# Attention and a gated layer in windows: the second window's weights in another order, its sums kept in SBUF, copies a step later, tiles moved to multiples of 512 bytes

## The chip, the core and the metric

One core of a Trainium2 chip runs one program. The metric is the device time of that program in microseconds (us); lower is better. TensorE (PE) multiplies, VectorE (DVE) and ScalarE (ACT) work on tiles in SBUF and PSUM, GpSimd (POOL) and SyncE (SP) here mostly issue DMA transfers between DRAM and SBUF. Each engine takes its instructions strictly in the order of its own queue and waits where an input isn't there.

## The reference

Linear attention on 8 batches of 576 tokens with 8 heads of 64, then a gated layer on the 4608 token rows of 512:

```python
q_s = softmax(q, axis=-1); k_s = softmax(k, axis=2)       # k: over the 576 positions
kv = np.einsum('bhsd,bhse->bhde', k_s, v)
x = np.einsum('bhsd,bhde->bhse', q_s, kv)                   # then laid out as [4608, 512]
gate = 1.0 / (1.0 + np.exp(-(x @ w_gate)))                  # w_gate, w_val: [512, 1536]
out = gate * (x @ w_val) @ w_out                            # w_out: [1536, 512]
```

The weights come in as 64-bit floats and are narrowed to 32 bits on the chip.

## The kernel before

The tokens are cut into 9 windows of 512 (w = 0 to 8; the title's spans). The columns of the gate and value weights are cut into 12 blocks j of 128, or 6 pairs p of two blocks.

Window 0 runs in 12 steps j with plain float32 matmuls. In step j, `g1_0(j)` (L594) makes gate and value columns in two PSUM tiles `gv` out of a ring of three; `g_sig_0` (ACT, L602) takes the sigmoid of the one, `g_mul_0` (DVE, L606) multiplies it by the other, which frees the tiles for the steps after; and `g2_0(j-1)` (PE, L621) multiplies the result of the step before with the output weights. Beside it, three kinds of work prepare the windows to come. Weights are narrowed: `w_low` and `w_join` on DVE (L131, L153), `w_top` on ACT (L138, L146), the same as `wo_low`, `wo_join`, `wo_top` for the output weights. `wo_save(j)` splits the output weights of step j into a high part (ACT copy, L195) and a low part (DVE subtraction, L196), both fp32r, in a tile `wo_hl` (two buffers in turn), and POOL saves them to DRAM. `w_sums(p)` (DVE, L226) and `split_w(p)` (ACT casts L213, DVE subtractions L214) form for a pair four sums S1 to S4 of weight blocks, for a scheme with seven instead of eight block products, and split sums and three plain blocks (`a_w`, kept in SBUF) into high and low parts. The sums of a pair are put in the one buffer `s_sb` and saved to DRAM; those of the last pair go through `wo_hl` instead. And `after_first(j)` runs the attention of window 1: maxima, exponentials and sums of k and q (`k_max`, `k_sub`, `k_exp`, `k_sum`, `qn_max`, `qn_sub`, `qn_exp`, `qn_sum`, `qf_mul`), `k_mm` and `k_done` for kv, transposes `qf_tr`, splits `qT_split`, `x_mm` and its evacuation `x_ev`, and at the end `c_subs` and `c_split`, which make the moving operands `c_hl` of the window.

Windows 1 to 8 have 6 steps p each. `g1(w, p)` (L639) makes seven products of 12 matmuls of 256 columns, in the order A11, S1, S2, A12, S3, S4, A22: three take their weights (the stationary operand) from `a_w`, four from `s_sb`; ACT and DVE empty PSUM into `sg` (L657 is the first copy). After each S product, `s_load` fetches that sum of the next step into `s_sb` (POOL, L260). `g2` (L702) makes 24 matmuls of 512 columns with the split products `h` as weights and `wo_hl` as moving operand; `wo_load` (POOL, L208) fetches `wo_hl` under two tags, one buffer pair that is called `wo_hl` and one called `wo_t`. `side_a` and `side_b` run the attention of the next window. Window 2's v tiles 2 to 4 take tiles of the `ring` of eleven 2 KB tiles; in the other windows they lie in `f_last`, which in window 0 holds the last pair's weights.

The order of every engine's work is the order in which the code is written (the scheduler is set to manual). The order of windows 1 to 8 is p = 0 to 5 in each.

As the program is built, nearly all large tiles start 64 or 0 bytes past a multiple of 128: `s_sb`, `kv_sb`, `f_last` and `ring` at 128 modulo 512 bytes of a partition, `c_hl`, `a_w`, `h`, `wo_hl` and `wo_t` at 448.

Of the kernel before, what the change touches and what calls it, by code (L numbers as in the profile page):

```python
# [51 lines left out]
def attn_moe(ctx: ExitStack, tc: tile.TileContext, qf, qn, qT, k, kT, v, wg, wv, wo, out):  # L52
# [138 lines left out]

    def wo_save(j):
        src = wo_t[j // 2][:, j % 2]
        t = two.tile([P, 2, DM], F32R, name="wo_hl")
        nc.scalar.copy(out=t[:, 0], in_=src)  # L195
# [55 lines left out]

    def s_save(p, src, i0, i1):
        n = 2 * DM
        nc.gpsimd.dma_start(
            out=s_dram[p][:, i0 * n:i1 * n], in_=src.rearrange("p s h e -> p (s h e)").bitcast(F32)
        )
# [437 lines left out]
    def g2(w, p):  # L694
        if p == 0:
            acc_new(w)
        h, o = h_hl.pop((w, p)), wo_hl.pop((w, p))
        for i in range(2):
            for m in range(NT):
                sl = slice(m * P, (m + 1) * P)  # L700
                for lh, rh in ((0, 0), (0, 1), (1, 0)):
                    nc.tensor.matmul(  # L702
                        acc[w][m], lhsT=h[lh][:, i, sl], rhs=o[i][:, rh],
                        start=(p == 0 and i == 0 and lh == 0 and rh == 0),
                        stop=(p == NS - 1 and i == 1 and lh == 1),
                    )
# [91 lines left out]
    def after_first(j):  # L800
# [17 lines left out]
        if j == 3:
            for hp in range(NP):
                k_sum(1, hp)  # L820
            for c in range(NC):
                qn_sum(1, c)
# [4 lines left out]
        if j == 4:
            k_done(1)
        if 4 <= j <= 7:
            qf_tr(1, j - 4, ps_gv.tile([P, T], F32, name="gv"))  # L830
        if 5 <= j <= 8:
            qT_split(1, j - 5)
# [246 lines left out]
```

## Time and profile before

| | |
|---|---|
| median of 3 runs | 1014.23 us (1014.09 to 1016.1) |
| profiled execution | 1016.99 us, of which the span from first to last instruction is 1015.2 us |
| mean granted TensorE clock | 0.975 |
| window 0 begins its first matmul L594 at | 35.29 us |
| window 1 begins at | 196.49 us |
| window 2 begins at | 317.21 us |

Rows of the trace give the start in us from the span's start, the duration, engine, line, operation, tiles (output <- inputs), shapes and how many instructions are merged in the row; in brackets stands the idle time of the engine before it and what ended that. Rows of stretches (from:to) give the length and then, engine by engine in the order PE, weight loads, DVE, ACT, POOL, the busy time with the number of instructions, then the granted clock, the DMA share and GB/s. A matmul's duration overlaps the next one's, so the pace of matmuls is read from start to start. Lines L are those of the kernel before.

### The profile page before, as it was taken

To read this page: it belongs to the slowest core of one execution; us is meant where nothing else is said; L and a number is where in the kernel's file an instruction comes from. 1 tells how busy PE (TensorE), PEld (TensorE's weight loads), DVE (VectorE), ACT (ScalarE), POOL (GpSimd) and SP (SyncE) were. 2 spreads that over 40 slices of the span, in tenths; PEclk is the share of its full clock that TensorE was granted. 3 is DMA by queue.
4 is the path that set the end of the run, shared out by engine and by line. 5 is a ranking of instruction groups with operands and counts; after the bars stand their busy time and mean duration, and the time that the engine had idled before them with its cause. 6 is when DMAs were issued, how large, how long until landed. Compare 5 with 4: busy or idle time off the path is not lost.

```text
span 1015.2 us, 15663 instructions
## 1 busy us (share of the span) xinstructions
PE 957.5 (94%) x6062; PEld 826.2 (81%) x6062; DVE 611.1 (60%) x1010; ACT 475.9 (47%) x815; POOL 171.2 (17%) x323
## 2 busy tenths in 40 slices
PE   5959899878899999999999999999999999999998
PEld 4525344468799999999999999999999999999997
DVE  8476967566266656666666656665665475464342
ACT  3639887345154535363446344633463344353222
POOL 0000001121112211211122111211221122212120
PEclk8979999979799999999999999999999999999999
DMA  9837756889569996899699968996999679868672
GB/s 334 320 106 272 267 222 172 309 266 339 153 207 208 371 322 205 230 365 313 199 248 358 310 200 262 353 300 203 277 340 275 214 203 340 244 184 249 205 208 83
DMA packets 94873, 259.88 MB, mean 256 GB/s; under 512 B 15376, under 2 KB 17680, under 8 KB 94160
## 3 DMA queue, kind: packets, MB, share of 16 engines
q0 software_dynamic: 44720, 170.42, 54.7%
q1 hardware_dynamic: 50080, 88.48, 29.3%
q8 instruction: 48, 0.79, 0.4%
q14 instruction: 25, 0.20, 0.1%
HBM read 230.29 MB, written 28.56 MB: 255 GB/s over the span
## 4 chain that ended last, share of the span: by engine, by line
PE 76%; DMA 8%; ACT 8%; DVE 5%; issue 3%; POOL 1%; SPq 0%; POOLq 0%; DVEq 0%; ACTq 0%
PE gv L639 43%; PE acc L702 22%; PE gv L594 3%; PE at L362 3%; DMA kmax_row<-k_max 2%; PE acc L621 2%; PE gv L522 2%; ACT ring L341 1%; DMA s<-s_sb 1%; ACT ring L441 1%; DMA q_m_row<-q_m 1%; DMA ring<-v_in 1%; DMA ring<-qT_in 1%; ACT kt L295 1%; DMA q_b<-q_m_row 1%
## 5 line engine op out<-in xcount | busy, mean ns | idle before, releaser
L639 PE MATMUL gv<-c_hl,s_sb 128*128 128x256 f32 x2304 | 283.0, 278 | 12.3 <-ACT sg L657 12.2
L639 PEld LDWEIGHTS gv<-c_hl,s_sb 128*128 128x128 f32 x2304 | 272.5, 189 | 14.7 <-ACT sg L657 14.1
L702 PE MATMUL acc<-wo_hl,h 128*128 128x512 f32 x1152 | 272.8, 393 | 0.0
L702 PEld LDWEIGHTS acc<-wo_hl,h 128*128 128x128 f32 x1152 | 214.7, 189 | 43.7 <-issue 0.2
L639 PE MATMUL gv<-c_hl,a_w 128*128 128x256 f32 x1728 | 231.9, 284 | 0.0
L639 PEld LDWEIGHTS gv<-c_hl,a_w 128*128 128x128 f32 x1728 | 220.2, 192 | 4.1 <-issue 1.0
L260 POOL DMA_DIRECT2D s_sb<-s x192 | 102.2, 533 | 327.1 <-PE gv L639 321.5
L665 DVE TENSOR_TENSOR sg<-gv,sg 128x512 f32<-128x512 f32 x48 | 33.2, 691 | 177.7 <-PE gv L639 177.7
L208 POOL DMA_DIRECT2D wo_hl<-wo x96 | 51.1, 533 | 310.4 <-PE acc L702 307.7
L594 PE MATMUL gv<-x,f_w 128*128 128x512 f32 x160 | 72.7, 607 | 9.5 <-ACT h L602 5.6
L667 ACT COPY sg<-gv 128x512 f32<-128x512 f32 x48 | 28.2, 587 | 107.0 <-PE gv L639 107.0
L657 ACT COPY sg<-gv 128x512 f32<-128x512 f32 x48 | 28.0, 584 | 97.7 <-PE gv L639 73.3
L594 PEld LDWEIGHTS gv<-x,f_w 128*128 128x128 f32 x160 | 30.4, 194 | 47.4 <-issue 34.4
L669 DVE TENSOR_TENSOR sg<-sg 128x512 f32<-128x512 f32 x48 | 33.2, 693 | 57.1 <-ACT sg L667 57.1
L621 PE MATMUL acc<-wo_t,h 128*128 128x512 f32 x96 | 47.3, 639 | 14.1 <-DVE h L606 14.1
L690 DVE TENSOR_TENSOR h<-sg,h 128x1024 fp32r<-128x1024 f32 x48 | 58.8, 1226 | 1.6
L672 ACT ACTIVATE sg<-sg 128x512 f32<-128x512 f32 x48 | 30.4, 632 | 54.0 <-DVE sg L671 54.0
L678 DVE TENSOR_TENSOR sg<-sg 128x512 f32<-128x512 f32 x48 | 33.2, 693 | 33.5 <-ACT sg L672 33.5
L621 PEld LDWEIGHTS acc<-wo_t,h 128*128 128x128 f32 x96 | 19.3, 205 | 40.4 <-issue 23.8
L662 ACT COPY sg<-gv 128x512 f32<-128x512 f32 x48 | 28.2, 587 | 44.4 <-PE gv L639 44.4
L659 ACT COPY sg<-gv 128x512 f32<-128x512 f32 x48 | 28.1, 586 | 26.1 <-PE gv L639 26.0
L396 ACT CAST kv_sb<-kmax_b 64x256 fp32r<-64x256 f32 x14 | 5.7, 404 | 66.5 <-DVE kmax_b L372 66.1
(155 smaller groups left out, 1056.1 us busy)
## 6 DMA issues: line engine op xcount, KB each, us to landing
s_sb<-s POOLq DMA_DIRECT2D x192, 512.0 KB, 7.1
wo_hl<-wo POOLq DMA_DIRECT2D x96, 512.0 KB, 5.7
s<-s_sb POOLq DMA_DIRECT2D x5, 2048.0 KB, 8.1
out<-x SPq DMA_DIRECT2D x36, 256.0 KB, 8.8
ring<-k_in SPq DMA_DIRECT2D x28, 256.0 KB, 14.3
ring<-qn_in SPq DMA_DIRECT2D x28, 256.0 KB, 10.4
q_b<-q_m_row SPq DMA_DIRECT2D x56, 128.0 KB, 8.7
ring<-qT_in SPq DMA_DIRECT2D x28, 256.0 KB, 9.0
```

The costliest lines, as they stand in the source:

```text
L208: nc.gpsimd.dma_start(out=t.rearrange("p h e -> p (h e)"), in_=wo_dram[2 * p + i].bitcast(F32R))
L260: nc.gpsimd.dma_start(out=s_sb[:, i].rearrange("p h n e -> p (h n e)"), in_=s_dram[p][:, i * n:(i + 1) * n].bitcast(F32R),)
L362: nc.tensor.matmul(kvps[b][:, hp], lhsT=kt[:n, sl], rhs=vt[:n, sl], start=(t == 0 and hp == 0), stop=(t == len(KTILES) - 1 and hp == NP - ...
L594: nc.tensor.matmul(ps[n], lhsT=w[:, kt // 2, sl], rhs=x_0[:, kt], start=(kt == 0), stop=(kt == NK - 1),)
L621: nc.tensor.matmul(acc[0][m], lhsT=h_0[j][:, m * P:(m + 1) * P], rhs=wo_t[j // 2][:, j % 2], start=(j == 0), stop=(j == NJ - 1),)
L639: nc.tensor.matmul(ps[:, n], lhsT=lh(kt), rhs=c_hl[i][:, x, kt], start=(first and n == 0 and kt == 0 and lh is wh and x == 0), stop=(last ...
L665: nc.vector.tensor_tensor(out=sg[:, 0], in0=rr, in1=sg[:, 0], op=ALU.add)
L669: nc.vector.tensor_tensor(out=sg[:, 3], in0=sg[:, 3], in1=sg[:, 2], op=ALU.add)
L672: nc.scalar.activation(sg[:, 0:2, 0], sg[:, 0:2, 0], AF.Sigmoid)
L678: tt(out=sg[:, 0:2, 0], in0=sg[:, 0:2, 0], in1=sg[:, 0:2, 1], op=ALU.mult)
L690: nc.vector.tensor_tensor(out=lo, in0=sg[:, :, 0], in1=hi.bitcast(F32), op=ALU.subtract)
L702: nc.tensor.matmul(acc[w][m], lhsT=h[lh][:, i, sl], rhs=o[i][:, rh], start=(p == 0 and i == 0 and lh == 0 and rh == 0), stop=(p == NS - 1 ...
```

## The change

- Window 1 takes its pairs in the order 5, 0, 1, 2, 3, 4 (`step`), the output weights likewise. The last pair's sums go to `s_sb` like the others and are still there when window 1 begins with that pair; they are saved to DRAM from there.
- `split_w(p)` and `w_sums(p)` have fixed steps: sums in even steps, split in the odd step after; the last split is in step 11.
- The high copy of the output weights (`wo_hi`) and `wo_save` run one step later, `wo_low` one step earlier; `wo_top(j+1)` stays in step j but stands ahead of the sigmoid there.
- The attention of window 1 is spread otherwise over the steps (`after_first`, `beside_first`); `x_ev`, `k_done` and `qT_split` stand at the head of a step, before the narrowing.
- Window 2's v tiles 2 to 4 lie in `f_last`, loaded in step 11.
- Three unused tiles shift the others: every tile named above now starts at a multiple of 512 bytes, except the buffer pair called `wo_hl`, which as built starts at 192 modulo 512.

```diff
+    pad = ctx.enter_context(tc.tile_pool(name="pad", bufs=1))
+    pad.tile([P, 80], F32, name="pad_2")
...
+    const.tile([P, 96], F32, name="pad_0")
     s_sb = const.tile([P, 4, 2, 2, 2 * P], F32R, name="s_sb")
...
+    const.tile([P, 48], F32, name="pad_1")
...
+    wo_out = {}
+    def wo_hi(j):
+        wo_out[j] = t = two.tile([P, 2, DM], F32R, name="wo_hl")
+        nc.scalar.copy(out=t[:, 0], in_=wo_t[j // 2][:, j % 2])
+
     def wo_save(j):
-        src = wo_t[j // 2][:, j % 2]
-        t = two.tile([P, 2, DM], F32R, name="wo_hl")
-        nc.scalar.copy(out=t[:, 0], in_=src)
+        t = wo_out.pop(j)
         nc.vector.tensor_tensor(
...
         for i, t in enumerate(s_32.pop(p)):
-            if p < NS - 1:
-                o = s[:, i:i + 1]
-            else:
-                o = two.tile([P, 1, 2, DM], F32R, name="wo_hl", tag="wo_hl")
-            parts(o, t)
-            if p == NS - 1:
-                s_save(p, o, i, i + 1)
-        if p < NS - 1:
-            s_save(p, s, 0, 4)
+            parts(s[:, i:i + 1], t)
+        nc.gpsimd.dma_start(
+            out=s_dram[p], in_=s_sb.rearrange("p s h n e -> p (s h n e)").bitcast(F32)
+        )
...
+    def step(w, i):
+        return (i - 1) % NS if w == 1 else i
...
+    def beside_first(j):
+        if j == 6:
+            k_done(1)
+        if 7 <= j <= 10:
+            x_ev(1, j - 7)
+        if 6 <= j <= 9:
+            qT_split(1, j - 6)
...
             if t < 2:
                 vt = v_two[t]
-            elif b == 2:
-                vt = ring.tile([P, DM], F32, name="ring")
             else:
                 vt = f_last[:, t - 2].rearrange("p n e -> p (n e)")
...
         if j == 10:
+            c_subs()
+            load_next(1, 5, range(2))
             for i in (B11, T1, T2, B21):
                 c_split(i)
-            load_next(1, 5)
-            for i in range(4):
-                s_load(0, i)
+        if j == 11:
+            for t in range(2, 5):
+                v_load(2, t)
...
     for j in range(NJ):
         g1_0(j)
+        beside_first(j)
+        if j > 0:
+            wo_hi(j - 1)
         if j + 2 < NJ:
             w_top(j + 2)
         if j + 1 < NJ:
             w_join(j + 1)
+        if j + 1 < NJ:
+            wo_top(j + 1)
         wo_join(j)
...
-        if j + 1 < NJ:
-            wo_low(j + 1)
+        if j + 2 < NJ:
+            wo_low(j + 2)
         g_sig_0(j)
-        wo_save(j)
+        if j > 0:
+            wo_save(j - 1)
...
-        if j - 1 in sums:
-            split_w(sums[j - 1])
-        if j + 1 < NJ:
-            wo_top(j + 1)
-        if j in sums:
-            w_sums(sums[j])
+        if j % 2:
+            split_w(j // 2)
+        else:
+            w_sums(j // 2)
```

The steps j of window 0 in which `after_first` issues the attention of window 1:

| work | before | after |
|---|---|---|
| qn_max, qn_sub, qn_exp, qn_sum | 0, 1, 2, 3 | 1, 2, 2, 3 |
| k_max (with its trip through DRAM) | 0 | 0 |
| k_sub, k_exp, k_sum | 1, 2, 3 | 3, 4, 2 |
| qf_mul, k_mm | 3, 3 | 4, 5 |
| qf_tr, x_mm (one a step) | 4 to 7, 6 to 9 | 5 to 8, 6 to 9 |
| c_subs | 9 | 10 |

What stands on the engines' queues at three places. First DVE in steps 0 and 1 of window 0, before (f_w, wo_t: narrowed weights; h_0: the gate product of g_mul; k_max, k_neg, q_m: maxima of k and q), from the last of the k maxima:

```order
L288 TENSOR_REDUCE k_max_376<-lent_127 128x1
L289 TENSOR_SCALAR k_neg_377<-k_max_376 128x1
L430 TENSOR_REDUCE q_m_390<-ring_158 128x8
L430 TENSOR_REDUCE q_m_390<-ring_160 128x8
L430 TENSOR_REDUCE q_m_390<-ring_162 128x8
L430 TENSOR_REDUCE q_m_390<-ring_164 128x8
L153 SCALAR_TENSOR_TENSOR f_w_351<-f_w_351,sg_85 128x2x256 x2
L153 SCALAR_TENSOR_TENSOR wo_t_333<-wo_t_333,wo_raw_148 128x512
L606 TENSOR_TENSOR h_0_359<-gv_341,h_0_359 128x512
```

and after, from g_mul of step 0 on, ahead of which stand the same k maxima and joins (wo_hl: the subtraction of wo_save; s_sb, a_w: those of split_w(0)):

```order
L602 TENSOR_TENSOR h_0_368<-gv_348,h_0_368 128x512
L136 TENSOR_SCALAR w_raw_344<-w_raw_344 128x1024
L136 TENSOR_SCALAR wo_raw_370<-wo_raw_370 128x512
L205 TENSOR_TENSOR wo_hl_411<-wo_t_339,wo_hl_411 128x512
L223 TENSOR_TENSOR s_sb_88<-s_32_375,s_sb_88 128x512
L223 TENSOR_TENSOR s_sb_88<-s_32_376,s_sb_88 128x512
L223 TENSOR_TENSOR s_sb_88<-s_32_377,s_sb_88 128x512
L223 TENSOR_TENSOR s_sb_88<-s_32_378,s_sb_88 128x512
L223 TENSOR_TENSOR a_w_433<-f_w_246,a_w_433 128x2x512
L223 TENSOR_TENSOR a_w_433<-f_w_246,a_w_433 128x512
L426 TENSOR_REDUCE q_m_455<-ring_164 128x8
L426 TENSOR_REDUCE q_m_455<-ring_166 128x8
```

The four maxima of q (q_m) move from ahead of the row h_0_359 (g_mul of step 0) to behind the row h_0_368, its counterpart, and the copy's and the split's subtractions come between them.

Second ACT from the sigmoid of step 2 on (h_0_472 before, h_0_484 after), before (ring: q and k tiles, whose exponentials are L441 and, behind the piece shown, L341; s_sb, a_w: the split of pair 0):

```order
L602 ACTIVATE h_0_472<-gv_452 128x512
L195 CAST wo_hl_474<-wo_t_424 128x512
L213 CAST s_sb_83<-s_32_427 128x512
L213 CAST s_sb_83<-s_32_428 128x512
L213 CAST s_sb_83<-s_32_429 128x512
L213 CAST s_sb_83<-s_32_430 128x512
L213 CAST a_w_482<-f_w_240 128x2x512
L213 CAST a_w_482<-f_w_240 128x512
L138 ACTIVATE wo_raw_365<-wo_raw_365 128x512
L146 ACTIVATE wo_t_424<-wo_raw_365 128x512
L441 ACT_TABLE_LOAD
L441 ACTIVATE ring_158<-ring_158 128x512
```

and after, from the end of step 2 on, that is behind h_0_484 and the exponentials of q (L293: k_sum; L201: the high copy of output weights; L222: the split of pair 1):

```order
L293 ACTIVATE lent_133,k_sum_389<-lent_133,k_neg_388 128x576 x4
L201 CAST wo_hl_528<-wo_t_418 128x512
L143 ACTIVATE w_raw_372<-w_raw_372 128x1024
L151 ACTIVATE f_w_473<-w_raw_372 128x2x256 x2
L143 ACTIVATE wo_raw_429<-wo_raw_429 128x512
L151 ACTIVATE wo_t_535<-wo_raw_429 128x512
L598 ACT_TABLE_LOAD
L598 ACTIVATE h_0_542<-gv_518 128x512
L222 CAST s_sb_88<-s_32_492 128x512
L222 CAST s_sb_88<-s_32_493 128x512
L222 CAST s_sb_88<-s_32_494 128x512
L222 CAST s_sb_88<-s_32_495 128x512
```

The exponentials of k_sum now stand in step 2, ahead of the narrowing and the sigmoid h_0_542 of step 3, and the casts of the split behind that sigmoid; the split of pair 0 is done a step earlier.

Third ACT from the last sigmoid of window 0 (h_0_1069 before) to the first copy out of PSUM of window 1 (sg from gv), before:

```order
L602 ACTIVATE h_0_1069<-gv_1057 128x512
L195 CAST wo_hl_1071<-wo_t_961 128x512
L213 CAST wo_hl_1076<-s_32_1007 128x512
L213 CAST wo_hl_1080<-s_32_1008 128x512
L213 CAST wo_hl_1084<-s_32_1009 128x512
L213 CAST wo_hl_1088<-s_32_1010 128x512
L213 CAST a_w_1075<-f_last_92 128x2x512
L213 CAST a_w_1075<-f_last_92 128x512
L578 CAST c_hl_1101<-ring_980 128x512
L578 CAST c_hl_1101<-x_32_84 128x512
L578 CAST c_hl_1106<-ring_982 128x512
L657 COPY sg_85<-gv_1109 128x512
```

and after (last sigmoid h_0_1065):

```order
L598 ACTIVATE h_0_1065<-gv_1051 128x512
L222 CAST s_sb_88<-s_32_1001 128x512
L222 CAST s_sb_88<-s_32_1002 128x512
L222 CAST s_sb_88<-s_32_1003 128x512
L222 CAST s_sb_88<-s_32_1004 128x512
L222 CAST a_w_1069<-f_last_97 128x2x512
L222 CAST a_w_1069<-f_last_97 128x512
L201 CAST wo_hl_1090<-wo_t_943 128x512
L574 CAST c_hl_1093<-ring_1017 128x512
L574 CAST c_hl_1093<-x_32_89 128x512
L574 CAST c_hl_1098<-ring_1019 128x512
L653 COPY sg_90<-gv_1103 128x512
```

The four casts of the sums go to s_sb instead of to four wo_hl tiles, and the high copy of the last output weights comes behind them.

More of the change, by code (lines that the diff above doesn't have):

```diff
@@ L692, in h_split, with g2 @@
         )
-    def g2(w, p):
-        if p == 0:
+    def step(w, i):
+        return (i - 1) % NS if w == 1 else i
+    def g2(w, at):
+        p = step(w, at)
+        if at == 0:
             acc_new(w)
@@ L768, in side_b, with load_next @@
         load_next(n, p)
-    def load_next(n, p):
+    def load_next(n, p, vs=range(5)):
         if n + 1 >= NW:
@@ L794, in load_next @@
                     k_load(b, t)
-                for t in range(4 if b == 2 else 5):
+                for t in vs:
                     v_load(b, t)
+    def beside_first(j):
[5 more added lines that the diff above has]
+            qT_split(1, j - 6)
     def after_first(j):
@@ L805, in after_first @@
             k_max_read(1)
+        if j == 1:
             for c in range(NC):
                 qn_max(1, c)
-        if j == 1:
+        if j == 2:
             for c in range(NC):
                 qn_sub(1, c)
+            for c in range(NC):
+                qn_exp(1, c)
+            for hp in range(NP):
+                k_sum(1, hp)
+        if j == 3:
             for t in range(5):
                 k_sub(1, t)
-        if j == 2:
             for c in range(NC):
-                qn_exp(1, c)
+                qn_sum(1, c)
+        if j == 4:
             for t in range(5):
                 k_exp(1, t)
[L818 to L822, printed above, removed]
             for hp in range(NP):
                 qf_mul(1, hp)
+        if j == 5:
             for t in range(5):
                 k_mm(1, t)
[L827 to L832, printed above, removed]
         if 6 <= j <= 9:
             x_mm(1, j - 6)
-            x_ev(1, j - 6)
+        if 5 <= j <= 8:
+            qf_tr(1, j - 5, ps_gv.tile([P, T], F32, name="gv"))
         if j in (2, 4, 6, 8):
             load_next(1, j // 2)
-        if j == 9:
+        if j == 10:
             c_subs()
-        if j == 10:
+            load_next(1, 5, range(2))
             for i in (B11, T1, T2, B21):
                 c_split(i)
-            load_next(1, 5)
-            for i in range(4):
-                s_load(0, i)
+        if j == 11:
+            for t in range(2, 5):
+                v_load(2, t)
     def lend(i):
@@ L1012, in attn_moe @@
         after_first(j)
+    wo_hi(NJ - 1)
     g_mul_0(NJ - 1)
@@ L1016, in attn_moe, with wo_next @@
         c_split(i)
+    wo_save(NJ - 1)
+    def wo_next(w, at):
+        wo_load(w, step(w, at))
     prev = None
@@ L1019, in attn_moe @@
         last = w == NW - 1
-        for p in range(NS):
-            end = last and p == NS - 1
-            g1(w, p, None if end else (p + 1) % NS)
-            if p == NS - 1 and not last:
+        for at in range(NS):
+            p = step(w, at)
+            end = last and at == NS - 1
+            g1(w, p, None if end else step(w + (at + 1) // NS, (at + 1) % NS))
+            if at == NS - 1 and not last:
                 for i in range(7):
@@ L1027, in attn_moe @@
             if not last:
-                side_a(w + 1, p)
+                side_a(w + 1, at)
             if prev is None:
                 g2_0(NJ - 1)
-                wo_load(1, 0)
-                wo_load(1, 1)
+                wo_next(1, 0)
+                wo_next(1, 1)
             else:
                 g2(*prev)
-                if not (last and p >= NS - 1):
-                    wo_load(w + (p + 1) // NS, (p + 1) % NS)
-            prev = (w, p)
+                if not end:
+                    wo_next(w + (at + 1) // NS, (at + 1) % NS)
+            prev = (w, at)
             if not last:
-                side_b(w + 1, p)
+                side_b(w + 1, at)
     g2(*prev)
```

17 lines of the change are left out of this document (5 added, 12 removed).

## The prediction

> **What bounds the kernel now.** I read the busy table first, then windows of the span, then TensorE's rows in order of time, and at each of its gaps the rows of the engine that ended it.
>
> ```profile
> PE 957.5 (94%) x6062; PEld 826.2 (81%) x6062; DVE 611.1 (60%) x1010; ACT 475.9 (47%) x815; POOL 171.2 (17%) x323
> ...
> 200.00:225.00 25.00, 15.54 (x94) 13.62 (x95) 14.59 (x23) 11.16 (x20) 5.88 (x11) 0.80 0.68 222
> ...
> 350.00:450.00 100.00, 99.57 (x710) 93.08 (x709) 63.28 (x107) 45.80 (x85) 19.15 (x36) 1.00 0.96 281
> ```
>
> TensorE (PE) is the bound. From 350 us on it is busy 99.57 us of 100, and only a faster matmul could help there; DMA and the other engines are hidden. Before 300 us it waits: 15.54 us busy in one slice of 25. Its rows (start, duration, in brackets the idle time ahead and what ended it):
>
> ```profile
> 47.49 3.70 PE L594 MATMUL gv<-x,f_w 128*128 128x512 f32 x8 [1.74 <-ACT h L602]
> 59.19 5.87 PE L621 MATMUL acc<-wo_t,h 128*128 128x512 f32 x8 [7.99 <-DVE h L606]
> 77.08 5.40 PE L621 MATMUL acc<-wo_t,h 128*128 128x512 f32 x8 [5.16 <-DVE h L606]
> ...
> 89.18 3.60 PE L621 MATMUL acc<-wo_t,h 128*128 128x512 f32 x8
> ...
> 105.45 3.70 PE L621 MATMUL acc<-wo_t,h 128*128 128x512 f32 x8 [0.96 <-DVE h L606]
> 116.86 5.40 PE L594 MATMUL gv<-x,f_w 128*128 128x512 f32 x8 [3.83 <-ACT h L602]
> 138.77 7.13 PE L594 MATMUL gv<-x,f_w 128*128 128x512 f32 x16 [0.96 <-DVE ring L498]
> 153.70 7.13 PE L594 MATMUL gv<-x,f_w 128*128 128x512 f32 x16 [2.97 <-DVE ring L498]
> ...
> 196.49 1.99 PE L639 MATMUL gv<-c_hl,a_w 128*128 128x256 f32 x12
> 209.46 2.93 PE L639 MATMUL gv<-c_hl,s_sb 128*128 128x256 f32 x12 [9.62 <-ACT sg L657]
> 212.19 2.29 PE L639 MATMUL gv<-c_hl,a_w 128*128 128x256 f32 x12
> ...
> 258.40 2.08 PE L362 MATMUL at<-ring 64*128 64x128 f32 x8 [6.83 <-DMA ring<-v_in]
> 260.41 7.86 PE L702 MATMUL acc<-wo_hl,h 128*128 128x512 f32 x24
> 268.10 1.59 PE L639 MATMUL gv<-c_hl,a_w 128*128 128x256 f32 x12
> 269.53 2.88 PE L639 MATMUL gv<-c_hl,s_sb 128*128 128x256 f32 x24
> 272.25 1.60 PE L639 MATMUL gv<-c_hl,a_w 128*128 128x256 f32 x12
> 273.69 2.88 PE L639 MATMUL gv<-c_hl,s_sb 128*128 128x256 f32 x24
> ...
> 277.85 5.63 PE L702 MATMUL acc<-wo_hl,h 128*128 128x512 f32 x24
> 500.31 2.31 PE L522 MATMUL gv<-ring,kv_sb 128*128 128x256 f32 x18
> 502.46 0.88 PE L522 MATMUL at<-ring,kv_sb 128*128 128x256 f32 x6
> ```
>
> The gaps sum to 40 us. After a gap of 3.83 us or more the next eight matmul records take 5.4 to 5.9 us instead of 3.6: about 2 us more each; after 2.97 us nothing of the kind shows.
>
> **The change, part by part.** I follow each queue in order with the starts of the rows below as unit costs (start to next start); an instruction begins when its engine is free and its inputs are there.
>
> ```profile
> 54.27 2.46 DVE L430 TENSOR_REDUCE q_m<-ring 128x8 f32<-128x512 f32 x4
> 56.65 1.28 DVE L153 SCALAR_TENSOR_TENSOR f_w<-f_w,sg 128x512 int32<-128x512 int32 x2
> ...
> 71.52 3.09 DVE L336 TENSOR_TENSOR ring<-ring,kmax_b 128x512 f32<-128x512 f32 x5 [5.92 <-DMA kmax_b<-kmax_row]
> ...
> 106.85 2.50 DVE L214 TENSOR_TENSOR s_sb<-s,s_sb 128x512 fp32r<-128x512 f32 x4
> 109.26 1.83 DVE L214 TENSOR_TENSOR a_w<-f_w,a_w 128x1024 fp32r<-128x1024 f32 x2
> 97.25 0.78 ACT L295 ACTIVATE lent<-lent,k_neg 128x576 f32<-128x576 f32 x1
> ...
> 100.29 2.48 ACT L138 ACTIVATE sg<-sg 128x1024 f16<-128x1024 f32 x1
> 103.81 1.28 ACT L602 ACT_TABLE_LOAD   x1
> ...
> 105.59 0.61 ACT L195 CAST wo_hl<-wo_t 128x512 fp32r<-128x512 f32 x1
> 106.10 2.18 ACT L213 CAST s_sb<-s 128x512 fp32r<-128x512 f32 x4
> 109.65 1.35 ACT L138 ACTIVATE wo_raw<-wo_raw 128x512 f16<-128x512 f32 x1
> 110.74 0.72 ACT L146 ACTIVATE wo_t<-wo_raw 128x512 f32<-128x512 f32 x1
> ...
> 200.53 0.62 ACT L213 CAST wo_hl<-s 128x512 fp32r<-128x512 f32 x1 [8.68 <-DMA wo<-wo_hl]
> 248.92 0.48 SPq L331 DMA_DIRECT2D ring<-v_in  x1
> 176.43 0.54 POOL L254 DMA_DIRECT2D s<-s_sb  x1
> ...
> 187.77 2.14 POOL L260 DMA_DIRECT2D s_sb<-s  x4 [4.48 <-DMA s<-s_sb]
> s_sb<-s POOLq DMA_DIRECT2D x192, 512.0 KB, 7.1
> ```
>
> *Steps 0 and 1 (1.74 + 7.99 + 2.27 slow clock = 12.0 us now).* wo_top(1), 1.7 us of ACT (L138 with its L146), now stands ahead of the sigmoid of step 0, so PE's first gap grows to 3.4. The four maxima of L430 (2.4 us) leave DVE's queue ahead of g_mul(0), and so does the copy's subtraction, which waited for ACT: g_mul(0) ends near 56.2 instead of 59.1, while PE, 1.7 later, is ready at 52.8. Gaps 3.4 + 3.4, and slow clock between 0 and 3.6 since both lie between the 2.97 that was free and the 3.83 that was not; I take 1.8. Sum 8.6: gain 3.4. [...]
>
> *Step 2 (5.16 + 1.8 = 7.0).* k_sub, whose five subtractions stood ahead of g_mul(1) and waited 5.92 us for kmax_b, moves two steps on, where kmax_b is long there. DVE has g_mul(1) at 66.7, PE asks for it at 67.5. Gain 7.0. On POOL's queue the round trip of the key maxima, over at 71.5 in the row above, now stands ahead of the first save of output weights; that save's buffer is next wanted at 77, so the delay hides.
>
> *Step 4: a new wait.* k_sum (4 activations, 3.0 us from 97.25 to 100.29) comes onto ACT in step 2 behind exponentials that wait for DVE's subtractions, so ACT enters step 3 at 76.7. There follow wo_hi 0.5, w_top 3.4, wo_top 1.7, table 1.3, sigmoid 0.5, and only at 84.1 the casts of split_w(1). DVE, idle since 77.9, then has split 4.2, k_sub 3.0, qn_sum 3.0 (four reductions like L430's and two small operations), the joins 1.8 and g_mul(3) 0.7 to 97.5. PE wants g_mul(3) at 88.6: 8.9 us, and 2.3 of slow clock. Before: 0.96. Loss 10.2. k_mm, taken from step 3 to step 5, only changes its place on PE.
>
> *Steps 5 to 9 (3.83 + 1.8 + 0.96 + 2.97 = 9.6).* x_ev and the split of the transposed q move from behind x_mm of their step to the head of the next. I find 1.5, 0.35, 0.2 and 0.35 left, each a g_mul that comes just too late: gain 7.2.
>
> *From window 0 to window 1 (9.62 + 1.43 + 0.69 = 11.7).* Before, the last split goes through the two-buffer wo_hl tile, so that ACT waits 8.68 us at 200.53 for a DMA, with the evacuation of the first product (L657) queued behind it. Now the four sums go to s_sb, free since about 180 (save of pair 4 issued at 168.5, 11.3 to land as from 176.43 to 187.77), and nothing in that chain waits for a transfer. I get the split done on DVE at 190.3, PE ready at 192.1, ACT free at 191.2: no gap. Gain 11.7. In exchange s_sb[S1] for the next step can be fetched only when the 2 MB save of pair 5, issued at 188.6, has landed: near 199.9; with 7.1 of its own it is there at 207.0, wanted at 206.8. I take 0, and up to 4.
>
> *The v tile of window 2 (6.83 + 2.23 = 9.1).* Its fifth DMA was issued at 248.92 behind a ring tile and landed at 258.4. Now it goes into f_last, right after split_w(5) has read it at 190: some 40 us early. Gain 9.1.
>
> Sum of waits: 3.4 + 7.0 - 10.2 + 7.2 + 11.7 + 9.1 = 28.2. If wait and reload come out badly (step 4 at 13, reload 4) it is 20; without the new wait 38.
>
> *The starts of tiles.* No row shows a tile at 0 mod 512, so this is bounded by the nearest. Per matmul of 256 columns, start to start, with the residue of weights and moving operand modulo 512: s_sb 128 with c_hl 448: (272.25 - 269.53)/24 = 113.3 ns. a_w 448 with c_hl 448: (273.69 - 272.25)/12 = 120.0. kv_sb 128 with ring 128: (502.46 - 500.31)/18 = 119.4. So two operands in the same place modulo 128 run at 120, two that differ at 113.3: 6.7 ns less. After the change s_sb and c_hl are both at 0, as kv_sb and ring are alike now: nearest to that row, 120. That is 2304 x 6.7 ns = 15.4 us lost. g2 (L702) has 448 with 448 now; after, its h is at 0 and one of its two wo_hl tiles at 192, which differ modulo 128: half of 1152 x 6.7 ns = 3.8 gained. a_w stays alike. Net loss 11.6. Ends: nothing from any of it (0), or everything at the better pace, a_w 1728 x 6.7 = 11.5 and L702 7.7, a gain of 19. [...]
>
> All in all 28.2 - 11.6 = 16.6 us. The profiled execution took 1016.99 (span 1015.2), 2.8 above the median 1014.23, which I count from: 997.6, told as 998.
>
> **Rivals.**
> - *The pace doesn't depend on starts* (113.3 stays for another reason, such as where s_sb lies): 1014.2 - 28.2 = 986. For it: two kinds of row differ in more than a residue. [...] 0.18.
> - *Multiples of 512 are the good place for all*: 1014.2 - 28.2 - 19 = 967. For it: weights are read in rows of 512 bytes, and none is now read without crossing such a multiple. Against: 128 with 128, the nearest, is a slow one. 0.12.
> - *Slower: that same alignment costs every matmul one more 6.7 ns*, with s_sb two: 5184 x 6.7 + 15.4 = 50, so 1014 - 28 + 50 = 1036. It decides from 28.2/5184 = 5.4 ns a matmul. Against: no row of 256 columns is above 120. 0.07.
> - *New waits take the gains*: the step 4 wait and the reload of s_sb worse than worked out, waits give 10 to 18, pace as in mine: 1008 to 1016. For it: the reload's margin is nil by the 11.3 us row. 0.13.
>
> **How the numbers follow.** Mine has 0.50, and 992 to 1004 for itself. The range 978 to 1010 holds it, the unchanged pace and most of the new waits; left out are 0.12 below and about 0.07 above. A measurement tells about 0.2% (2 us) here. Faster: 0.50 + 0.18 + 0.12 + 0.08 = 0.88; same 0.04; slower 0.08.
>
> **What would show it.** PE idle near 59 and 77 gone or short, a new gap of about 9 us ended by g_mul (DVE, L602 in the changed kernel) in step 4; no gap in the first step of window 1 nor ahead of its k_mm; the rows of 24 s_sb matmuls (L635 there) 2.86 us from start to start where now 2.72, a_w unchanged at 1.44, g2 5.39 where now 5.47. I am wrong if s_sb keeps 2.72, if a_w moves, or if step 4 has no gap.

## The result, and the profile after

The changed kernel took 999.91 us, median of five runs (998.38 to 1000.17); the kernel before took 1014.23 beside it (1013.74 to 1019.4). The ratio is 0.985 with a 95% interval of 0.9824 to 0.9875: 1.5% faster. The profiled execution took 999.88, its span 998.0.

The busy table and the two windows of the span that were shown of before:

```profile
PE 964.4 (97%) x6062; PEld 832.2 (83%) x6062; DVE 610.5 (61%) x1010; ACT 475.7 (48%) x815; POOL 167.4 (17%) x316
...
200.00:225.00 25.00, 24.73 (x184) 23.48 (x183) 17.49 (x30) 14.93 (x27) 5.32 (x10) 1.00 1.15 353
350.00:450.00 100.00, 99.50 (x698) 92.99 (x697) 61.97 (x104) 44.82 (x83) 18.55 (x35) 1.00 0.97 272
```

The slice from 200 to 225 us, in which TensorE worked 15.54 us before, is full. From 350 us on TensorE is as busy as it was, but fits 698 matmuls into 100 us where it had 710: each costs more on the average. TensorE's rows in order of time, with its gaps in brackets:

```profile
33.85 10.46 PE L590 MATMUL gv<-x,f_w 128*128 128x512 f32 x24
47.77 5.40 PE L590 MATMUL gv<-x,f_w 128*128 128x512 f32 x8 [3.45 <-ACT h L598]
54.89 3.70 PE L617 MATMUL acc<-wo_t,h 128*128 128x512 f32 x8 [1.72 <-DVE h L602]
...
75.77 3.60 PE L617 MATMUL acc<-wo_t,h 128*128 128x512 f32 x8
...
84.01 3.70 PE L590 MATMUL gv<-x,f_w 128*128 128x512 f32 x8 [1.21 <-ACT h L598]
97.21 6.68 PE L617 MATMUL acc<-wo_t,h 128*128 128x512 f32 x8 [9.50 <-DVE h L602]
...
185.76 2.00 PE L635 MATMUL gv<-c_hl,a_w 128*128 128x256 f32 x12
187.59 3.04 PE L635 MATMUL gv<-c_hl,s_sb 128*128 128x256 f32 x24
...
201.10 3.04 PE L635 MATMUL gv<-c_hl,s_sb 128*128 128x256 f32 x24
...
236.28 1.60 PE L635 MATMUL gv<-c_hl,a_w 128*128 128x256 f32 x12
...
307.93 3.04 PE L635 MATMUL gv<-c_hl,s_sb 128*128 128x256 f32 x24
310.81 1.60 PE L635 MATMUL gv<-c_hl,a_w 128*128 128x256 f32 x12
312.25 5.71 PE L703 MATMUL acc<-wo_hl,h 128*128 128x512 f32 x24
315.06 2.90 PE L703 MATMUL acc<-wo_hl,h 128*128 128x512 f32 x12
317.80 1.59 PE L635 MATMUL gv<-c_hl,a_w 128*128 128x256 f32 x12
...
183.42 0.53 POOL L250 DMA_DIRECT2D s<-s_sb  x1 [4.14 <-DVE s_sb L223]
191.91 0.54 POOL L258 DMA_DIRECT2D s_sb<-s  x1 [2.89 <-DMA s<-s_sb]
```

(The row at 315.06 is the second half of the one at 312.25.) The last two rows are POOL's save of pair 5's sums and the first reload. The gaps near 59 and 77, in the first step of window 1 and ahead of its k_mm are gone or short; one of 9.50 us is new. The spacing, start to start: s_sb (310.81 - 307.93)/24 = 120.0 ns where it was 113.3; a_w 1.44/12 = 120.0 as before; g2 (315.06 - 312.25)/12 = 234 in its first half, whose moving tile is the wo_hl pair, and 228 in the second.

Three stretches of the two traces show where the 17.1 us between the profiled executions went:

| stretch of TensorE's rows | before | after | gain |
|---|---|---|---|
| to the first a_w row of window 1 | 196.49 | 185.76 | 10.7 |
| from there, three steps | 71.6 | 50.5 | 21.1 |
| from the fourth step to the end | 743.4 | 758.1 | -14.6 |

So the waits gave 32 to 33 us (the last row's loss is in the three steps too, about 0.9), and the longer spacing took about 15.6. From the fourth step on, and from start to start, the s_sb matmuls take 251.1 us before and 262.0 after, those of g2 251.8 and 255.4, and all others the same to 0.1 us.

### The profile page after: what moved, and what is told of

Read it like the earlier page. It is cut to its first block, busy times and chain, and to the rows that moved or that the text cites. A ratio compares the mean times of both kernels' runs of the same rounds, so it can differ in the third digit from the quotient of the medians.

```text
span 998.0 us, 15641 instructions
## 1 busy us (share of the span) xinstructions
PE 964.4 (97%) x6062; PEld 832.2 (83%) x6062; DVE 610.5 (61%) x1010; ACT 475.7 (48%) x815; POOL 167.4 (17%) x316
## 4 chain that ended last, share of the span: by engine, by line
PE 84%; ACT 8%; DMA 5%; DVE 2%; issue 1%; SPq 0%; ACTq 0%; DVEq 0%
PE gv L635 46%; PE acc L703 23%; PE gv L590 5%; PE acc L617 3%; PE at L358 3%; PE gv L518 2%; ACT ring L337 2%; DMA sg<-wv_in 1%; ACT ring L437 1%; DMA lent<-kT_in 1%; PE at L518 1%; ACT kt L293 1%; DMA ring<-k_in 1%; ACT L437 1%; DMA lent<-v_in 1%
## 5 line engine op out<-in xcount | busy, mean ns | idle before, releaser
L635 PE MATMUL gv<-c_hl,s_sb 128*128 128x256 f32 x2304 | 293.6, 283 | 1.8 <-ACT sg L653 1.8
L635 PEld LDWEIGHTS gv<-c_hl,s_sb 128*128 128x128 f32 x2304 | 283.6, 192 | 3.1 <-ACT sg L653 3.1
L258 POOL DMA_DIRECT2D s_sb<-s x188 | 99.7, 530 | 330.1 <-PE gv L635 327.1
L661 DVE TENSOR_TENSOR sg<-gv,sg 128x512 f32<-128x512 f32 x48 | 33.2, 691 | 188.1 <-PE gv L635 188.1
L663 ACT COPY sg<-gv 128x512 f32<-128x512 f32 x48 | 28.2, 587 | 110.1 <-PE gv L635 110.1
L658 ACT COPY sg<-gv 128x512 f32<-128x512 f32 x48 | 28.2, 587 | 43.6 <-PE gv L635 43.6
L667 DVE TENSOR_TENSOR sg<-gv,sg 128x512 f32<-128x512 f32 x48 | 33.2, 692 | 6.2
```

Source lines behind the costliest of these rows:

```text
L258: nc.gpsimd.dma_start(out=s_sb[:, i].rearrange("p h n e -> p (h n e)"), in_=s_dram[p][:, i * n:(i + 1) * n].bitcast(F32R),)
L635: nc.tensor.matmul(ps[:, n], lhsT=lh(kt), rhs=c_hl[i][:, x, kt], start=(first and n == 0 and kt == 0 and lh is wh and x == 0), stop=(last ...
L661: nc.vector.tensor_tensor(out=sg[:, 0], in0=rr, in1=sg[:, 0], op=ALU.add)
L667: nc.vector.tensor_tensor(out=sg[:, 1], in0=z, in1=sg[:, 1], op=ALU.add)
```

## The experiments

The kernel before, which ran beside each group, took 1014 to 1021 us by the group. So ratios are compared between groups, and where a few us matter, stretches of the traces. Those repeat well: the changed kernel and the run without the wait of step 4, whose code is the same from window 1 on, were run in different groups and both need 808.59 us from there to TensorE's last row.

**The parts that remove waits, one at a time.** First the order of window 1 and the way of the last split were put back, with all else as changed.

```diff
-        return (i - 1) % NS if w == 1 else i
+        return i
 ...
-            parts(s[:, i:i + 1], t)
+            if p < NS - 1:
+                o = s[:, i:i + 1]
+            else:
+                o = two.tile([P, 1, 2, DM], F32R, name="wo_hl", tag="wo_hl")
+            parts(o, t)
```

> The changed kernel with the order of window 1 and the way of the last split as they were before: pair 0 first, the sums of pair 5 through the two-buffer wo_hl tile to DRAM. All else, pads too, as changed. Theory: ACT again waits some 8.7 us for a transfer with the evacuation of the first product behind it, and the 11.7 us of gaps in the first step of window 1 come back: 1011 to 1013 us by the ratio of the changed kernel. Rival (the gap would have gone anyway, with the copies of output weights a step later and the loads moved): 1000.

It took 1011.69 us, ratio 0.991 (0.9878 to 0.9942). The rows of ACT and PE in the first step of window 1:

```profile
189.34 0.62 ACT L222 CAST wo_hl<-s 128x512 fp32r<-128x512 f32 x1 [8.14 <-DMA wo<-wo_hl]
194.10 0.62 ACT L222 CAST wo_hl<-s 128x512 fp32r<-128x512 f32 x1 [2.91 <-DMA s<-wo_hl]
198.80 2.93 PE L646 MATMUL gv<-c_hl,s_sb 128*128 128x256 f32 x12 [9.08 <-ACT sg L664]
```

The chain is back link by link: a cast waits for a buffer's save, the evacuation (L664) stands behind it, and TensorE behind that. From window 1's first row to the end it needs 820.2 us where the changed kernel needs 808.6: 11.6, and the theory had 11.7. (By the ratios it would be 6 us, 0.991 for 0.985; the kernel before was at its slowest, 1021, in this group.) Then the v tile alone was put back into the ring.

```diff
+            elif b == 2 and t == 4:
+                vt = ring.tile([P, DM], F32, name="ring")
 ...
-            for t in range(2, 5):
+            for t in range(2, 4):
                 v_load(2, t)
 ...
                 kT_load(b, 0); kT_load(b, 1)
+                if b == 3:
+                    v_load(2, 4)
```

> The changed kernel with the last v tile of window 2 loaded again as before: into a ring tile, issued on SP in step 1 of window 1 behind the loads of kt, and not into f_last at the end of window 0. Theory (that tile's late transfer made the gap ahead of k_mm in the second step): the tile is issued some 6 us before it is wanted and lands after 9 to 12, so PE waits 4 to 7 us ahead of the last k_mm matmuls and up to 2 us more are lost to the slow clock behind: 1004 to 1009 us by the ratio of the changed kernel (0.985), that is a ratio of 0.989 to 0.994. Rival (the gap went because window 1 has another order): 0.985.

It took 1007.0 us, ratio 0.9884 (0.9864 to 0.9904), just under the 0.989 to 0.994 of the theory. SP's row of the issue and TensorE's behind it:

```profile
222.54 0.58 SPq L329 DMA_DIRECT2D ring<-v_in  x1
236.22 2.07 PE L360 MATMUL at<-ring 64*128 64x128 f32 x8 [5.36 <-DMA ring<-v_in]
238.22 7.04 PE L705 MATMUL acc<-wo_hl,h 128*128 128x512 f32 x24
```

5.36 us of gap, and 24 matmuls in 7.04 us instead of 5.71: the same stretch is 816.2, 7.6 us longer. Each gap is back with its own part and stays away with the other, so both rivals are out and the two parts are separate.

**The new wait of step 4.** DVE sat idle for 6.77 us in step 3 of the changed kernel, since its next work in order was the split behind ACT's casts, and only then did k_sub, qn_sum and the joins ahead of g_mul(3) come:

```profile
84.50 2.50 DVE L223 TENSOR_TENSOR s_sb<-s,s_sb 128x512 fp32r<-128x512 f32 x4 [6.77 <-ACT s_sb L222]
87.00 1.83 DVE L223 TENSOR_TENSOR a_w<-f_w,a_w 128x1024 fp32r<-128x1024 f32 x2
88.74 3.08 DVE L332 TENSOR_TENSOR ring<-ring,kmax_b 128x512 f32<-128x512 f32 x5
...
96.47 0.68 DVE L602 TENSOR_TENSOR h<-gv,h 128x512 f32<-128x512 f32 x1
```

The experiment fills that idle time and lets the split's subtractions wait.

```diff
             g_mul_0(j - 1)
+        if j == 4:
+            split_lo(1)          # DVE's part of split_w(1), and its save
 ...
+        if j == 3:
+            for t in range(5):
+                k_sub(1, t)
+            for c in range(NC):
+                qn_sum(1, c)
+            split_hi(1)          # ACT's part of split_w(1)
-        if j % 2:
+        elif j % 2:
             split_w(j // 2)
```

> The changed kernel with the wait of step 4 taken out by order alone: in step 3 k_sub and qn_sum go ahead of the split on DVE, into the 6.8 us in which DVE waits for ACT's casts, and the split's six subtractions on DVE go behind g_mul(3) in step 4 (the casts on ACT stay). Theory (the queue of DVE makes that gap): g_mul(3) ends near 86.4 us, PE wants it at 87.7, so the gap of 9.5 and the 3.0 of slow clock behind it go; 0 to 4 us come back as gaps of steps 5 to 9, which the later PE covers now: 987 to 991 us. Rival (ACT is the bound of these steps and the gap only moves on): 996 to 1000.

It took 990.24 us, ratio 0.9738 (0.9712 to 0.9764).

```profile
85.16 0.67 DVE L624 TENSOR_TENSOR h<-gv,h 128x512 f32<-128x512 f32 x1
87.37 3.60 PE L639 MATMUL acc<-wo_t,h 128*128 128x512 f32 x8
100.61 3.70 PE L639 MATMUL acc<-wo_t,h 128*128 128x512 f32 x8 [2.78 <-DVE h L624]
```

g_mul(3) runs at 85.16 instead of 96.47 and TensorE doesn't wait for it. 2.78 us come back one step later, where the split's subtractions now stand on DVE with w_sums, qf_mul and two maxima ahead of g_mul(4); the clock does not slow behind this gap (3.70 for eight). Window 1 begins at 176.1, 9.6 us earlier, and the rest is as long as it was (808.6). DVE's order made the wait, not a lack of ACT's time.

**The pads.** First all three taken out, and then all three put alone into the kernel before.

```diff
-    pad.tile([P, 80], F32, name="pad_2")
-    const.tile([P, 96], F32, name="pad_0")
-    const.tile([P, 48], F32, name="pad_1")
```

> The changed kernel without its three pads: s_sb is back at 128 mod 512 and c_hl, a_w, h and the wo_t pair at 448, the wo_hl pair at 128; the order of work is that of the changed kernel. Theory A (spacing follows the distance from the weights' start to the moving tile's start, mod 512: 0 gives 120.0 and 226.7 ns, 320 gives 113.3, 192 gives 233.3): s_sb rows back to 113.3 ns, a_w 120.0, g2 still 226.7 and 233.3; time 999.9 - 2304 x 6.7 ns = 984.5 us. Theory B (as recorded: two operands that differ modulo 128 are short): s_sb 113.3 and the wo_hl half of g2 at 220, which takes another 576 x 13.3 ns = 7.7: 976.8 us. Rival (the pads have nothing to do with the pace): s_sb stays at 120 and the time at 999.9.

990.99 us, ratio 0.9736 (0.9711 to 0.9762). Rows of a plain step, and one of a step with a new wait:

```profile
407.16 2.88 PE L631 MATMUL gv<-c_hl,s_sb 128*128 128x256 f32 x24
409.88 1.60 PE L631 MATMUL gv<-c_hl,a_w 128*128 128x256 f32 x12
411.31 5.71 PE L699 MATMUL acc<-wo_hl,h 128*128 128x512 f32 x24
...
542.94 1.69 PE L631 MATMUL gv<-c_hl,s_sb 128*128 128x256 f32 x12 [1.38 <-ACT sg L649]
...
537.85 2.72 DVE L465 TENSOR_TENSOR ring<-ring,q_b 128x512 f32<-128x512 f32 x4 [6.15 <-DMA ring<-qT_in]
541.42 0.86 ACT L388 CAST kv_sb<-kmax_b 64x256 fp32r<-64x256 f32 x2 [12.53 <-DVE kmax_b L364]
```

s_sb is back at (409.88 - 407.16)/24 = 113.3 ns, and the wo_hl half of g2, at 128 with h at 448, stays at 234.0 (the median of its first halves): theory A's pace, and theory B's 220 is wrong. The time fell by less than 15.4. From the fourth step on the trace is 7.8 us shorter (750.3 for 758.1) where 2160 matmuls at 6.7 ns would give 14.4. Half of what is missing is new gaps, because the faster steps meet a transfer: DVE waits 6.15 us for the transposed q, k_done is queued behind it, ACT's cast of kv_sb behind that, and then the evacuation that TensorE needs. TensorE's gaps behind ACT sum to 5.0 us where the changed kernel has 1.8. The rest are s_sb matmuls that start 116 to 228 ns after the one ahead.

> The kernel before with the three pads and nothing else of the change: s_sb, c_hl, a_w, h and, other than in the changed kernel, both pairs of wo_hl tiles at 0 mod 512. Theory (the starts set the spacing of s_sb): s_sb 120.0 ns for 113.3, a_w 120.0 and g2 about 227 to 228 in both halves as before, no wait changed: 2304 x 6.7 ns = 15.4 us slower, a ratio of 1.015 to the kernel before. Rival (the longer spacing of the changed kernel comes from its other order of work): s_sb stays at 113.3 and the ratio is 1.000.

1026.76 us, ratio 1.0095 (1.0068 to 1.0121).

```profile
402.32 3.04 PE L643 MATMUL gv<-c_hl,s_sb 128*128 128x256 f32 x24
405.20 1.60 PE L643 MATMUL gv<-c_hl,a_w 128*128 128x256 f32 x12
...
207.37 2.93 PE L643 MATMUL gv<-c_hl,s_sb 128*128 128x256 f32 x12 [7.68 <-ACT sg L661]
255.10 2.07 PE L366 MATMUL at<-ring 64*128 64x128 f32 x8 [4.55 <-DMA ring<-v_in]
```

s_sb runs at 120.0 in the old order of work too, so the starts alone do it; the rival is out. But the cost is 8.2 us between the two profiled spans, not 15.4. From the fourth step on the trace is 11.8 longer (755.2 for 743.4), since the kernel before was not always at 113.3: of its 2160 s_sb matmuls in these steps some 190 lie 116 to 121 ns apart (below), which is worth 1.0 us, and what intervals of 140 ns and more, gaps included, take beyond the plain spacing is 5.4 us, against 3.6 with the pads. And the two waits in window 1 shrank from 9.62 and 6.83 to 7.68 and 4.55: my sentence that no wait would change was wrong.

**Which starts are slow.** Four layouts of the changed kernel, with pads of other sizes and all of a pool's tiles shifted together, give two or three new distances each. They took 991.56, 990.75, 997.36 and 991.11 us, one run each, and are read for the spacing alone.

> The changed kernel with other pads, for the spacing of matmuls alone. Starts mod 512: s_sb 128, c_hl 0, a_w 64, h 64, the wo_t pair 128, the wo_hl pair 384. Theory B (differ modulo 128: short): s_sb 120.0 ns, a_w 113.3, g2 220 in both halves. Theory A (distance mod 512 from weights to moving tile; only 0, 192, 256, 320 are known): the wo_hl half of g2, at distance 320, at 220; distances 384 (s_sb), 448 (a_w) and 64 (wo_t half) are new, each between 113.3 and 123.3, or 220 and 233.3. Rival (each tile's own start decides): s_sb as in the kernel before, 113.3.

> As the run before, with starts mod 512: s_sb 128, c_hl 64, a_w 192, h 192, the wo_t pair 320, the wo_hl pair 256. Theory B: s_sb 113.3 ns, a_w 120.0, g2 226.7 in the wo_t half and 220 in the wo_hl half. Theory A: s_sb, at distance 448, as a_w of the run before; a_w, at distance 384, as s_sb of that run; the wo_hl half, at distance 64, as the wo_t half of that run; the wo_t half, at distance 128, is new. Rival (each tile's own start decides): s_sb 113.3, and no such agreement between the two runs.

> The changed kernel with other pads, starts mod 512: s_sb 128, c_hl 192, a_w 448, h 448, the wo_t pair 192, the wo_hl pair 384. Distances (moving tile less weights, mod 512): s_sb 64, a_w 256, g2 256 in the wo_t half and 448 in the wo_hl half. For the 256-column matmuls the rows so far (mean start to start) are 120.0 ns at distance 0, 118.2 and 118.5 at 384, 113.5 and 114.9 at 448, 113.3 at 320; theory B (alike modulo 128 is slow) gives 113.3 to 115 for s_sb and 118 to 120 for a_w. Theory A (distance mod 512) says nothing of these two beforehand. For g2 the rows are 226.7 to 228.3 at 0, 229 to 230 at 64 and 320, 233 at 128, 234 at 192: theory B has failed there, and I expect 228 to 234 in both halves.

> As the run before, starts mod 512: s_sb 128, c_hl 320, a_w 192, h 192, the wo_t pair 64, the wo_hl pair 256. Distances: s_sb 192, a_w 128, g2 384 in the wo_t half and 64 in the wo_hl half. Theory B: s_sb 113.3 to 115 ns, a_w 118 to 120. Theory A: the wo_hl half, at 64 as twice before, 229.8; the others are new.

The spacings of these four traces and of all those above, as the median over steps from 350 us on, by the distance from the start of the weights to that of the moving tile, modulo 512 bytes:

| distance | 256 columns, ns | 512 columns (g2), ns |
|---|---|---|
| 0 | 119.9, 120.0 | 226.7 to 228.3; first half 228.9 |
| 64 | 113.3 | 228.9; first half 229.8 |
| 128 | 118.1 | 232.9 |
| 192 | 113.5 | first half 234.0 |
| 256 | 119.9 | 228.3 |
| 320 | 113.3 | first half 229.8 |
| 384 | 118.2, 118.3 | 232.9 |
| 448 | 113.5, 114.9 | first half 234.0 |

For 256 columns theory B told all of these: multiples of 128 were slow (118 to 120), odd multiples of 64 fast (113 to 115). For 512 columns it was otherwise: the rows repeat modulo 256, 0 and 256 were the best places (226.7 to 228.3), and 128 and 384 (232.9) and 192 and 448 (234.0) the slow ones. (A half that comes first in g2 has some 1 to 2 ns more, as the rows at 0 and 64 show.) The rival that a tile's own start decides is out: s_sb stands at 128 in all four layouts and runs at 118.3, 113.5, 113.3 and 113.5 ns.

**All distances made fast, and what came of it.** The order of step 4 as above, and a_w moved to 320 as well.

> The changed kernel with the order of step 4 as in the run without that wait, and other pads: s_sb and a_w both at 128 with c_hl at 448 (distance 320), h and both pairs of wo_hl tiles at 128 (distance 0). Theory (spacing follows the starts, TensorE is the bound): s_sb 113.3, a_w 113.3, g2 226.7 in both halves; from the run without pads, 991.0, less 9.6 for step 4, 1728 x 6.7 ns = 11.5 for a_w and 576 x 7.3 ns = 4.2 for g2: 966 us. Rival (the transfers are the next bound): without pads TensorE already waits 1.38 us near 543 and 1.08 near 747 for work that a late transfer of the transposed q holds up, at 0.98 of the DMA engines; those waits grow and the time is 972 to 982.

986.51 us, ratio 0.9661 (0.9632 to 0.969): no better pace, though s_sb and c_hl start where they start without pads. From the fourth step on it needs 751.5 us, 1.2 more than without pads, and not 15 less; the gaps, 5.7 us in all for 5.2, did not grow as the rival had it. Two steps of it:

```profile
402.21 2.99 PE L655 MATMUL gv<-c_hl,s_sb 128*128 128x256 f32 x24
405.04 1.57 PE L655 MATMUL gv<-c_hl,a_w 128*128 128x256 f32 x12
...
334.83 1.63 PE L655 MATMUL gv<-c_hl,s_sb 128*128 128x256 f32 x12 [2.07 <-ACT sg L673]
336.30 1.52 PE L655 MATMUL gv<-c_hl,a_w 128*128 128x256 f32 x12
337.66 2.88 PE L655 MATMUL gv<-c_hl,s_sb 128*128 128x256 f32 x24
340.38 1.52 PE L655 MATMUL gv<-c_hl,a_w 128*128 128x256 f32 x12
```

(405.04 - 402.21)/24 = 117.9 ns in one step, and (340.38 - 337.66)/24 = 113.3 in another, with the same tiles; after a gap of 2.07 us TensorE stays in the short spacing to the end of the step, and then falls back. So this layout had two steady spacings, 117.9 and 113.3 ns. What decides between them is not shown: of the nine gaps in the windows of this trace, four (0.40, 2.07, 0.40 and 0.40 us) are followed by the short spacing and five (0.20 to 0.76 us) by the long one, and each time the long one is back behind the next g2. The trace of before shows two spacings too, there the longer one after a gap of 0.43 us.

```profile
451.80 1.69 PE L639 MATMUL gv<-c_hl,s_sb 128*128 128x256 f32 x12 [0.43 <-ACT sg L657]
...
454.76 2.99 PE L639 MATMUL gv<-c_hl,s_sb 128*128 128x256 f32 x24
457.58 1.59 PE L639 MATMUL gv<-c_hl,a_w 128*128 128x256 f32 x12
```

(457.58 - 454.76)/24 = 117.5, where plain steps have 113.3. Last, a layout with s_sb and a_w at the distances of the second of the four layouts (448 and 384), where 62 of 70 plain s_sb rows were short, and both halves of g2 at 0, with two more changes of order:

```diff
-            for hp in range(NP):
-                qf_mul(1, hp)
 ...
+            if j == 5:
+                for hp in range(NP):
+                    qf_mul(1, hp)
             split_w(j // 2)
 ...
                     k_mm(b, t)
+                k_done(b)
             for hp in range(NP):
                 qT_sub(n, hp)
-            if b is not None:
-                k_done(b)
```

> The changed kernel with the starts that gave the shortest steady rows so far and three changes of order. Starts mod 512: s_sb 128, c_hl 64, a_w 192, h and both wo_hl pairs 192: s_sb 113.5 ns, a_w 118.2, g2 about 227 to 229 in both halves. Order: step 4 as in the run without that wait; qf_mul (2.5 us of DVE) moved from step 4 into the wait of 3.4 us that DVE has in step 5, so that the 2.78 us left ahead of g2_0(4) go; in the windows k_done goes ahead of qT_sub on DVE, so that a late transposed q no longer holds up the casts of kv_sb on ACT and the evacuation behind them (PE's gaps of 0.2 to 2.1 us in the runs with short rows). Theory: less than the run without pads (991.0, ratio 0.9736) by 9.6 + 2.8 for the start, 576 x 7 ns = 4.0 for g2, 2.9 for a_w and about 3 for the gaps: 22 us, a ratio of 0.952. Rival (the two operands' phase settles at the long spacing again, as in the run with a_w and s_sb both at distance 320, where rows of 117.8 and of 113.3 stand side by side): ratio 0.962 to 0.967.

976.49 us, ratio 0.9601 (0.9574 to 0.9628): 4.0% faster than the kernel before, and the best of all.

```profile
99.83 3.70 PE L638 MATMUL acc<-wo_t,h 128*128 128x512 f32 x8 [0.38 <-DVE h L623]
114.57 5.40 PE L611 MATMUL gv<-x,f_w 128*128 128x512 f32 x8 [2.35 <-DVE ring L515]
...
399.27 2.88 PE L656 MATMUL gv<-c_hl,s_sb 128*128 128x256 f32 x24
402.00 1.58 PE L656 MATMUL gv<-c_hl,a_w 128*128 128x256 f32 x12
```

No gap in the windows is longer than 0.62 us, and from the fourth step of window 1 on the kernel needs 742.6 us, 15.5 less than the changed one. The ratio is between theory and rival. Beside the run without pads, 2 of the 8 us that the theory lacks are in the windows (7.9 of 9.9 gained) and 6 in window 0 (6.1 of 12.4, from its first f_w row to window 1). There 2.35 us came back at the head of step 6: TensorE, now earlier, needs a gv buffer that DVE's split of the transposed q (L515) frees, and that stands behind k_done and split_w(2), which itself waits 3.42 us for ACT's casts. Eight matmuls at a slow clock follow (5.40 for 3.60). Another 1.4 us were never there to gain, as the slow row of step 4 took only 5.27 us without pads (6.68 in the changed kernel).

## Why the prediction was right, and where it was not

Between the two profiled executions the gain is 17.1 us where 16.6 were told. That they agree so well is luck: the waits gave some 4.5 us more than the 28.2 told, 1.4 of it no effect of the change, and the pace took 4.0 more. The median came out 2 us above the forecast because the sum was worked out on a profile of before that was 2.8 us longer than the median, and then taken off the median. The way into window 1 with its order, the v tile, the wait of step 4 and the starts have runs of their own. The shares of steps 0 to 2 and 5 to 9 are read from the two traces. Step by step:

- **Steps 0 and 1**, forecast gain 3.4: 5.0. The first gap is 3.45 as told, with 1.8 of slow clock behind it (5.40 for 3.60); the second is 1.72 instead of 3.4 and without slow clock. The 1.8 was a guess halfway between none and both. All eleven kernels with the new order show that first gap, 3.45 to 3.48 us, each with a slow row (5.40) behind it; but the last kernel's gap of 2.35 is followed by a slow row too, and those of 2.78 and 2.97 are not, so no length alone decides it. What went with it in these traces stands below the list.
- **Step 2**, 7.0: the gap is gone, but 1.21 us are lost in step 3 (the row at 84.01), where the sigmoid comes late because k_sum stands on ACT ahead of it. I had followed k_sum only to g_mul(3).
- **Step 4**, loss 10.2: 9.50 in place of 0.96, and 3.0 of slow clock for 2.3, together 11.5. Mechanism and place as forecast.
- **Steps 5 to 9**, gain 7.2: all 9.6. The four short gaps that I had left do not show in the run without step 4's wait either, which has only its 2.78 in step 5: they were mis-sized, not covered. Another 1.4 us lie ahead of all this (33.85 for 35.29 at the start of the first f_w row); in the twelve profiles beside that of before this start lies anywhere from 33.8 to 35.9, so it is no effect of the change.
- **Window 0 to window 1**, 11.7: confirmed by its undoing (11.6). The reload of s_sb costs nothing, as taken: the save issued at 183.42 was over at 191.91, after 8.5 us and not 11.3, and a reload of 7.1 from there ends at 199.0, ahead of the s_sb row at 201.10.
- **The v tile**, 9.1: the step fell from 30.87 to 20.99, which is 9.9 us. Put back alone it costs 7.6, as its transfer is issued 8.3 us ahead of the wait in the new order (222.54 for 230.86), and 2.7 before (248.92 for 251.57).
- **The starts**, net loss 11.6: the sign and the cause are shown, the sizes were off. s_sb went to 120.0 as told, but its 15.4 were counted from 113.3 for every matmul, which before did not hold: the s_sb rows lost 10.9 us from the fourth step on, some 11.6 over all 48 steps (10.9 x 48/45), and with the pads alone 12.6 (11.8 x 48/45). For g2 the step failed: "two that differ at 113.3" was read from matmuls of 256 columns and carried to 512, where distance 192 gives 234 and not 220. g2 lost 3.7 us (3.9 over all steps) where I had a gain of 3.8.

**When the clock goes slow.** The granted clock is in each trace, and it changes only on a grid of 3.41 us that runs on through the trace: in that of the changed kernel it is 0.50 from 14.49, 48.63 and 93.00 us on, for 10.24, 3.41 and 10.24 us, which is 3, 1 and 3 steps of the grid, and the second and third of these times lie 10 and 23 steps behind the first. Here are two neighbouring stretches of that grid around the gap of 2.35 us in the last kernel, and two around that of 2.78 in the run without the wait of step 4 (length; busy time of TensorE; the granted clock is the third figure from the end):

```profile
111.48:114.89 3.41, 1.05 (x3) 0.30 (x2) 3.00 (x8) 2.47 (x5) 0.00 (x0) 1.00 0.99 418
114.89:118.30 3.41, 3.41 (x5) 1.35 (x4) 3.41 (x7) 3.41 (x4) 0.00 (x0) 0.50 0.50 168
...
95.72:99.13 3.41, 2.11 (x5) 0.57 (x3) 3.34 (x8) 3.41 (x6) 0.00 (x0) 1.00 0.39 161
99.13:102.54 3.41, 1.93 (x5) 0.98 (x6) 2.97 (x6) 3.41 (x5) 0.03 (x1) 1.00 0.46 101
```

The shorter gap lies within one stretch, of which TensorE idles 0.69, and the next stretch has half the clock; the longer one is cut by a border into 0.38 and 0.43, and no slow one follows. The first gap of the changed kernel fills 0.75 of a stretch. In all thirteen traces, from 34 to 960 us, every stretch at full clock in which TensorE idles for 0.58 or more (32 of them) is followed by a slow one, and none with 0.56 or less is. So the gap of 2.35 us had a slow stretch behind it and those of 2.78 and 2.97 (cut by a border into 0.47 and 0.40) had none, by where they fell on the grid, which the forecast could not know.

The rivals: that of an unchanged pace said 986. Without the effect of the starts the time would have been some 984 (999.9 less 15.6), and the run without pads came to 987 by its ratio (0.9736 of 1014.2); so that rival would have had the time nearly right, and the pace wrong. The others did not happen.

## What to carry to other kernels

An engine that idles for another's result in mid-queue, with work for the critical engine queued behind, can give its time back by order alone, here 9.6 us in step 4: look at what could go into that idle time, and what of the waiting work nobody needs yet. Where TensorE is the bound, read its spacing start to start, for each pair of weights and moving tile and each number of columns; here it moved with where the tiles start by up to 6% at 256 columns (113.3 to 120.0 ns) and 3% at 512 (226.7 to 234.0), and multiples of 512 bytes were a slow place for the former (119.9 to 120.0). The waits changed with the pace: without the pads TensorE's gaps behind ACT sum to 5.0 us where the changed kernel has 1.8, and with the pads alone the two waits of window 1 shrank by 1.94 and 2.28 us. So a gain in the pace and the waits behind it are not to be added as if they were apart.
